# Attention and an MLP on one core: chunks of the MLP that follow the batches, and a first batch whose weights stay fp32

## The chip, the cores and the metric

The kernel runs on one core of a Trainium2 chip. TensorE (PE) multiplies, VectorE (DVE), ScalarE (ACT) and GpSimd (POOL) work elementwise, and SyncE (SP) issues all DMAs of this kernel. The metric is the device time of one launch in microseconds; the change is judged by the median of several runs before against several after.

## The reference

Attention over 8 batches with 8 heads, 576 tokens and 64 columns a head, in which all weights below the row's maximum less tau are set to zero; then an MLP over the 4608 rows of 512 columns:

```python
scores = scale * np.matmul(q, k.transpose(0, 1, 3, 2))
thresh = np.max(scores, axis=-1, keepdims=True) - tau
scores = np.where(scores >= thresh, scores, -1000000000.0)
scores = scores - np.max(scores, axis=-1, keepdims=True)
attn = np.exp(scores)
attn = attn / (np.sum(attn, axis=-1, keepdims=True) + 1e-09)
x = (attn @ v)              # to rows: (batch, token), columns: (head, 64)
h = x @ w_in                # 512 -> 2048
g = np.maximum(h, 0.0) + np.log1p(np.exp(-np.abs(h)))
out = g @ w_out             # 2048 -> 512
```

The two MLP weights arrive in 64-bit floats, q, k and v in 32-bit.

## The kernel before

**Units and tiles.** Two heads of one batch are a unit (32 units, four to a batch). A unit's scores are nine tiles of 128 query rows by 576 keys: four of the first 512 rows of each head, and one in the middle (tile 4) that holds the last 64 rows of both heads. The main loop (line 873) runs over the 288 tiles; within one it takes the steps of the string PAT in order, a letter each: high half, row maximum of the next tile, low half, transposes, exp, a part of the MLP, mask, another part, the extras, the scores of the tile after next, weight preparation, and the point at which deferred functions run. A function that is deferred by n runs at the n-th such point.

**One tile.** PE computes scores into one of two PSUM pairs (`scores`); DVE takes the row maximum (`row_max`), ACT the exp (`exps`), DVE applies the mask and sums the row (`mask`). POOL writes the weights' high half in fp16 (`weights_hi`, line 452), DVE the low half (`weights_lo`, line 457), and a DMA transposes both halves (`weights_T`); the halves lie in one of three buffers, `e16`. When a head is complete, PE multiplies the transposed halves by v, which is also split in two fp16 halves after a scaling (`top_v`, `split_v`, `values`); ACT and DVE add the two parts into `xp` (`values_out`). One unit's row sums become scales `R`, are written to DRAM and read back on 64 partitions each, POOL multiplies `xp` by them (`scale_x`, line 513), and three DMAs store it in DRAM (`store_x`). The q and k of the next unit are split in two parts, transposed on PE and copied by ACT on the way (`pre`).

**The MLP.** A chunk is 512 consecutive rows, nine in all, so a chunk straddles batches. `load_x` fetches it from DRAM, `split_x` scales it (ACT) and makes two fp16 halves (POOL). `hidden` (line 584) multiplies with w_in in three products (high by high, low by high, high by low), ACT computes softplus for two blocks at a time behind a table load, POOL splits the result into halves `g`, and `project` (line 646) multiplies with w_out; DVE adds the quarters of it up in `acc`. A generator, `stream`, yields after every matmul: one 512-column matmul is one unit of work, a chunk is 384 units. `target` says how many units are due at each tile: chunk 0 from tile 43, the next from 82, 118 and so on, one chunk for 36 tiles, 10.7 units a tile. Chunks 7 and 8 come after the last tile; they are called the tail and may use buffers that attention no longer needs.

**The weights.** Each of 32 pieces of 128 x 512 is read as words, one every second tile from tile 0. ACT, POOL and DVE turn them into fp32 (`to_f32`), DVE takes the maximum of each piece (`got`), four pieces make a block whose maximum gives its scale (`over_all`), then ACT scales and POOL splits it (`split`).

**Order.** DVE and ACT keep the program's order from tile 72 on (TQ); before that a scheduler orders the instructions of each engine. PE has four general PSUM banks (`ps_g`) for everything but the scores.

Of the kernel before, what the change touches and what calls it, by code (L numbers as in the profile page):

```python
# [24 lines left out]
P = 128  # L25
# [7 lines left out]
LAG0 = 7  # L33
PAT = "hRlTefmpfxSwp"
# [8 lines left out]
NW = 34  # L43
EB = 3
EXP = 0x7F800000
LAG = 10
NMM = 11.0
# [10 lines left out]
def tile_kernel(ctx: ExitStack, tc: tile.TileContext, q, k, v, tau, w_in, w_out, out):  # L58
# [53 lines left out]
    x_d = [dpool.tile([P, NPAIR, S], F32, name=f"x_d{b}") for b in range(B)]  # L112
# [60 lines left out]
    def over_all(name, cols, then):  # L173

        col = cpool.tile([P, 1], F32, tag="col", bufs=3, name=f"col_{name}")
        vec.reduce_max(col, cols, axis=AX.X)
# [18 lines left out]
    def to_f32(src, name, then):  # L195
# [21 lines left out]
        def second(m, n):  # L217
            mu = m.bitcast(U32)
            if n == 0:
                i = vec.tensor_scalar(out=mu, in0=mu, scalar1=3, scalar2=None, op0=ALU.logical_shift_left)  # L220
            elif n == 1:
# [27 lines left out]
    def prep_w(kind, g, n):  # L249

        ms, tops = blocks.setdefault((kind, g), ([], cpool.tile([P, 4], F32, tag="tops", bufs=3, name=f"tops_{kind}{g}")
                                                 if n == 0 else None))
# [27 lines left out]
        to_f32(src, f"{kind}{g}_{n}", got)  # L280
# [13 lines left out]
    for b in range(B):  # L294
        for hp in range(NPAIR):
            s = Unit()
            s.i, s.b, s.hp = len(units), b, hp
            s.r_d = dpool.tile([9, P], F32, name=f"r_d{s.i}")
            units.append(s)

    def load(s):
        h0 = 2 * s.hp
        s.kn = apool.tile([P, 10, D], F32, tag="nat", bufs=3, name=f"kn_{s.i}")
        s.qn = apool.tile([P, 10, D], F32, tag="nat", bufs=3, name=f"qn_{s.i}")
        for t, src in ((s.kn, k), (s.qn, q)):
            nc.sync.dma_start(
                t.rearrange("p (h s) d -> p h (s d)", h=2)[:, :, 0:NC * D],
                src[s.b, h0:h0 + 2, 0:SM, :].rearrange("h (p c) d -> p h (c d)", c=NC),
            )
# [15 lines left out]
    def top_v(s):  # L325
        tops = cpool.tile([P, 1], F32, tag="vtop", bufs=2, name=f"vtop_{s.i}")
        vec.tensor_reduce(tops, s.vn[0:P].rearrange("p h s d -> p (h s d)"), axis=AX.X, op=ALU.max,
                          apply_absolute_value=True)
# [12 lines left out]
        defer(1, spread)  # L341

    def split_v(s, j):
        if j == 0:
# [5 lines left out]
    def split_k(s):  # L350
# [3 lines left out]
        s.q2, s.kT, s.qT = [], [], []  # L354
# [87 lines left out]

    def mask(s, t):
# [3 lines left out]
            accum_out=s.sums[:, t:t + 1]))  # L447
# [12 lines left out]
    def weights_T(s, t):  # L460
# [4 lines left out]
        if t == M:  # L465
            nc.sync.dma_start_transpose(s.eT[0][:, :, SM:S], h[0:SR])
            nc.sync.dma_start_transpose(s.eT[1][:, :, 0:SR], h[SR:P])
            return
        j, c = divmod(t, NC + 1)
        c0 = j * SR + c * P  # L470
        nc.sync.dma_start_transpose(s.eT[j][:, :, c0:c0 + P], h)

    def values(s, g):
        if g == 0:
            s.xp = apool.tile([P, S], F32, tag="xp", name=f"xp_{s.i}")
# [15 lines left out]
    def row_scales(s):  # L491
        s.rs = apool.tile([P, 9], F32, tag="rs", name=f"rs_{s.i}")
        vec.tensor_scalar(out=s.rs, in0=s.sums, scalar1=1e-9, scalar2=v_scale[:, s.i:s.i + 1], op0=ALU.add, op1=ALU.mult)
# [7 lines left out]
    def row_scales_out(s, ps):  # L501
        rt = apool.tile([P, S], F32, tag="R", bufs=1, name=f"rt_{s.i}")[0:9, 0:P]
        act.activation(rt, ps[0:9, 0:P], AF.Copy, scale=2.0 ** -15)
        nc.sync.dma_start(s.r_d, rt)
        s.R = apool.tile([P, S], F32, tag="R", bufs=1, name=f"R_{s.i}")
        rows = s.r_d.rearrange("a p -> (a p)")
        for j in range(2):
            nc.sync.dma_start(s.R[j * D:(j + 1) * D, :], rows[j * S:(j + 1) * S].partition_broadcast(D))
        defer(XD, lambda: scale_x(s))
        defer(XD + 2, lambda: store_x(s))  # L510

    def scale_x(s):
        nc.gpsimd.tensor_tensor(out=s.xp, in0=s.xp, in1=s.R, op=ALU.mult)

    def store_x(s):
        for j, c0, n, t0 in ((0, 0, S, 0), (1, SR, SM, 0), (1, 0, SR, SM)):
            nc.sync.dma_start(x_d[s.b][j * D:(j + 1) * D, s.hp, t0:t0 + n], s.xp[j * D:(j + 1) * D, c0:c0 + n])
        ready.add(("x", s.b, s.hp))
# [5 lines left out]
    def load_x(u, cc):  # L524
        st = fpool.tile([P, TC], F32, tag="xst", name=f"xst_{u.n}_{cc}")
        u.st[cc] = st
        c = 0
        while c < u.T:
            b, o = divmod(u.t0 + c, S)
            m = min(S - o, u.T - c)  # L530
            need("x", b, cc)
            nc.sync.dma_start(st[:, c:c + m], x_d[b][:, cc, o:o + m])
            c += m

    def x_scale(u):
        n = NPAIR * ((u.t0 + u.T - 1) // S + 1)
        for i in range(n):
            need("v", i)
# [4 lines left out]
        vec.tensor_reduce(u.sx, v_scale[:, 0:n], axis=AX.X, op=ALU.min)  # L543
# [22 lines left out]
    def split_x(u, cc):  # L566
        if cc % 2 == 0:
            for l, tag in ((u.h, "xh"), (u.l, "xl")):
                t = fpool.tile([P, 2 * TC], F16, tag=tag, name=f"{tag}_{u.n}_{cc}")
                l += [t[:, i * TC:(i + 1) * TC] for i in range(2)]  # L570
        st = u.st.pop(cc)
# [3 lines left out]
    def hidden(u, fc):  # L575
# [4 lines left out]
        bank = ps_g.tile([P, TC], F32, tag="g", name=f"h_{u.n}_{fc}")  # L580
        e = slice(f * P, (f + 1) * P)
        for cc in range(NCC):
            for m, (i, x) in enumerate(((0, u.h), (0, u.l), (1, u.h))):
                nc.tensor.matmul(bank, wi[g, cc][:, i, e], x[cc], start=(cc == 0 and m == 0),  # L584
                                 stop=(cc == NCC - 1 and m == 2))
                if cc == NCC - 1 and m == 2:
                    u.full.append((fc, bank))
# [3 lines left out]
                yield 1.0  # L591
# [27 lines left out]
    def parts_of(u, fc, t):  # L619

        pool, tags, bufs = (fpool, ("gh", "gl"), NG)
        if u.tail:
            spare = [("kT", 2), ("qT0", 2), ("qT1", 2), ("nat", 3), ("e16", EB)]
# [7 lines left out]
        u.g[fc] = (gh, gl)  # L631
# [35 lines left out]
    def store_out(u, tb, a):  # L667
        t0 = u.t0 + tb * P
        c = 0
        while c < P:  # L670
            b, o = divmod(t0 + c, S)
            if o < SM:
                cg, p0 = divmod(o, P)
                m = min(P - p0, P - c)
                dst = out[b * S:b * S + SM, :].rearrange("(p c) e -> p c e", c=NC)[p0:p0 + m, cg, :]
            else:
                m = min(S - o, P - c)
                dst = out[b * S + o:b * S + o + m, :]
            nc.sync.dma_start(dst, a[c:c + m, :])
            c += m  # L680
# [29 lines left out]
    def stream():  # L710
# [4 lines left out]
        for it in order():  # L715
# [7 lines left out]
            if it[2:4] == (0 if u.tail else nq - 2, 0) and u.n + 1 < len(chunks):  # L723
                x_scale(chunks[u.n + 1])
            if it[4] >= 0:
# [7 lines left out]
                if it[4] == 0:  # L733
                    load_x(nx, 0)
# [32 lines left out]
    chunks, first = [], []  # L767
    while sum(u.T for u in chunks) < NT:
        u = Chunk()
        u.n, u.t0 = len(chunks), sum(c.T for c in chunks)  # L770
        u.T = TC
        u.h, u.l, u.acc, u.g, u.st, u.full = [], [], [], {}, {}, []
        u.scaled, u.unscaled = set(), set()
        b, o = divmod(u.t0 + u.T - 1, S)
        first.append((b + 1) * 9 * NPAIR + (LAG if chunks else LAG0))
        u.tail = first[-1] >= NS
# [3 lines left out]
    def target(g):  # L780

        done = 0
        for n, u in enumerate(chunks):
            work = 3 * NFC * (NCC * u.T / 512 + u.T / P)
            end = first[n + 1] if n + 1 < len(chunks) else 1 << 30
            if g < end:
                rate = work / (end - first[n])
                if n + 2 >= len(chunks) or end == first[n]:
                    rate = NMM
                return done + max(0, min(work, (g - first[n]) * rate))  # L790
            done += work
# [20 lines left out]
    def extras(i, t):  # L812
# [4 lines left out]
        for g, at_ in enumerate(VO):  # L817
            if at_ == t:
                values(cur, g)
            if at_ == 9 + t and prev:  # L820
                values(prev, g)
# [16 lines left out]
    for s in units:  # L838
        if s.i == 0:
            times = ((0, -1), (0, 0), (0, 3), (0, 4))  # L840
        elif s.i == 1:
            times = ((0, 4), (0, 6), (0, 8), (1, 0))
# [27 lines left out]
    scores(*tiles[1])  # L870

    done = 0.0
    for g, (cur, t) in enumerate(tiles):
# [6 lines left out]
        for step in PAT:  # L880
            if step == "T" and g:
                weights_T(*tiles[g - 1])
            elif step == "h":
                weights_hi(cur, t)
            elif step == "l" and g:
                weights_lo(*tiles[g - 1])
            elif step == "R" and nxt:
# [11 lines left out]
            elif step == "S" and g + 2 < NS:  # L899
                scores(*tiles[g + 2])  # L900
            elif step == "w":
# [46 lines left out]
```

## Time and profile before

| | |
|---|---|
| median of 3 runs | 1506.12 us (1504.12 to 1508.0) |
| the profiled execution | 1502.2 us |
| its span, first to last instruction | 1500.4 us |
| mean granted TensorE clock | 0.939 |
| DMA, share of 16 engines | 57.7% |

Durations and shares are of the profiled execution; its time is 1.8 us more than its span. A row of a view by windows gives, for a stretch of the span, its length, then for each engine the busy time and, in brackets, how many instructions ran, the granted clock, the share of time in which the DMA engines were busy, and the GB/s. A row of a group gives the line, the engine, the operation, what it writes and reads, the shape and the count; then the busy time and the mean of one in ns; then the idle time of the engine just before these instructions and who ended it. Line 147 is a helper through which all DVE and ACT operations pass, so those are told apart by names and shapes. A row of the waits gives who waited for whom, the time in all, how often and the longest.

### The profile page before, as it was taken

The numbers are of one execution on the slowest core, as the hardware profiler recorded it, in microseconds if no ns is written. First come the engines' busy times: TensorE is split into PE (matmuls) and PEld (weight loads), VectorE is DVE, ScalarE is ACT, GpSimd is POOL, SyncE is SP. The second block draws the span as 40 slices with busy tenths as digits, with TensorE's granted clock in tenths as the row PEclk, the third lists the DMA queues.
The fourth block names the chain that finished last, engine by engine and source line by source line (L and its number), as shares of the span: only waits on it lengthen the run. The fifth ranks groups of instructions, "written<-read, shape, count | busy, mean of one in ns | idle before, by whom it ended". The sixth has DMA issues, their size and how long they took to land.

```text
span 1500.4 us, 21721 instructions
## 1 busy us (share of the span) xinstructions
PE 1241.6 (83%) x6608; PEld 719.2 (48%) x6608; DVE 1062.1 (71%) x2113; ACT 819.9 (55%) x1305; POOL 987.9 (66%) x1097
## 2 busy tenths in 40 slices
PE   4554557877989988998898888998989889999998
PEld 3432334544555545554555545554555445444443
DVE  7897998998877887777777777787777767610101
ACT  4433446656566656665565656665766576442231
POOL 5477788887776667666766676667766775353531
PEclk9755659999999999999999999999999999999999
DMA  5877876755576656666765586666665756420101
GB/s 158 182 154 179 178 170 161 176 136 132 128 168 132 143 141 161 141 141 136 167 140 126 142 173 148 128 139 157 153 134 138 161 131 126 95 65 1 37 7 28
DMA packets 445317, 199.30 MB, mean 133 GB/s; under 512 B 376048, under 2 KB 419344, under 8 KB 445200
## 3 DMA queue, kind: packets, MB, share of 16 engines
q1 hardware_dynamic: 445200, 197.90, 57.7%
q8 instruction: 53, 0.87, 0.2%
q14 instruction: 64, 0.52, 0.1%
HBM read 73.40 MB, written 19.02 MB: 62 GB/s over the span
## 4 chain that ended last, share of the span: by engine, by line
DVE 24%; ACT 20%; PE 18%; issue 10%; POOL 10%; DMA 8%; SPq 3%; ACTq 0%; POOLq 0%; DVEq 0%
PE o L646 7%; PE h L584 7%; DVE negm L147 6%; DVE e_all L147 6%; ACT st L147 6%; ACT e_all L147 6%; ACT L147 5%; DMA eT<-e 3%; DVE e L147 3%; DVE acc L147 2%; DVE xp L147 2%; DMA vn<-in_v_dram 2%; PE s L429 2%; PE pv L480 1%; POOL g L171 1%
## 5 line engine op out<-in xcount | busy, mean ns | idle before, releaser
L646 PE MATMUL o<-w_o,g 128*128 128x512 f16 x1728 | 413.8, 384 | 21.6 <-POOL g L170 14.5
L452 POOL TENSOR_SCALAR e<-e_all 128x576 f16<-128x576 f32 x288 | 232.6, 808 | 279.0 <-DMA eT<-e 207.1
L147 ACT ACTIVATE e_all<-s,negm 128x576 f32<-128x576 f32 x288 | 213.0, 741 | 316.8 <-DVE negm L147 290.7
L584 PE MATMUL h<-xh,w_i 128*128 128x512 f16 x1152 | 374.2, 385 | 6.4 <-POOL xh L170 2.9
L429 PE MATMUL s<-kT,qT 128*128 128x288 f32 x1024 | 244.2, 354 | 119.4 <-DVE e_all L147 108.0
L147 DVE SCALAR_TENSOR_TENSOR e_all<-s,thr,e_all 128x576 f32<-128x576 f32 x288 | 233.7, 812 | 112.1 <-ACT e_all L147 111.6
L147 DVE SCALAR_TENSOR_TENSOR e<-e_all,e 128x576 f16<-128x576 f32 x288 | 276.9, 961 | 15.3 <-POOL e L452 14.2
L646 PEld LDWEIGHTS <-g 128*128 128x128 f16 x1728 | 158.7, 99 | 207.5 <-POOL g L170 20.1
L584 PEld LDWEIGHTS <-w_i 128*128 128x128 f16 x1728 | 161.0, 99 | 190.3 <-issue 17.8
L429 PEld LDWEIGHTS s<-kT,qT 128*128 128x128 f32 x1024 | 168.9, 208 | 172.4 <-DVE e_all L147 145.6
L147 DVE TENSOR_REDUCE negm<-s 128x1 f32<-128x576 f32 x288 | 215.5, 748 | 19.3 <-PE s L429 17.5
L584 PE MATMUL h<-xl,w_i 128*128 128x512 f16 x576 | 221.3, 384 | 4.8 <-POOL xl L171 4.8
L147 DVE SCALAR_TENSOR_TENSOR acc<-o,c,acc 128x512 f32<-128x512 f32 x108 | 79.6, 738 | 166.1 <-PE o L646 133.2
L480 PE MATMUL pv<-eT,vt 128*128 128x288 f16 x1152 | 179.6, 305 | 7.6 <-DMA eT<-e 6.8
L171 POOL TENSOR_TENSOR g<-st,g 128x512 f16<-128x512 f32 x144 | 169.9, 1181 | 8.3
L170 POOL TENSOR_SCALAR g<-st 128x512 f16<-128x512 f32 x144 | 99.9, 695 | 98.5 <-ACT st L147 96.2
L147 ACT ACT_TABLE_LOAD x109 | 139.8, 1283 | 27.6 <-DVE negm L147 26.0
L480 PEld LDWEIGHTS <-vt 128*128 128x128 f16 x1152 | 116.7, 104 | 64.4 <-issue 8.3
L147 ACT ACTIVATE st<-h,c 128x512 f32<-128x512 f32 x144 | 91.2, 684 | 87.6 <-PE h L584 87.0
L147 DVE TENSOR_TENSOR xp<-pv,xp 64x288 f32<-64x288 f32 x128 | 57.6, 450 | 94.9 <-ACT xp L147 93.2
L147 ACT ACTIVATE st<-st,c 128x512 f32<-128x512 f32 x144 | 96.1, 715 | 2.1
L171 POOL TENSOR_TENSOR vt<-vn,vt 128x576 f16<-128x576 f32 x64 | 84.6, 1321 | 1.8
(90 smaller groups left out, 1356.4 us busy)
## 6 DMA issues: line engine op xcount, KB each, us to landing
vn<-in_v_dram SPq DMA_DIRECT2D x128, 128.0 KB
qT<-qT SPq DMA_DIRECT2D x124, 128.0 KB
R<-r_d SPq DMA_DIRECT2D x64, 144.0 KB
kn<-in_k_dram SPq DMA_DIRECT2D x32, 256.0 KB
qn<-in_q_dram SPq DMA_DIRECT2D x32, 256.0 KB
wc_i<-in_moe_w_in_dram SPq DMA_DIRECT2D x16, 512.0 KB
wc_o<-in_moe_w_out_dram SPq DMA_DIRECT2D x16, 512.0 KB
eT<-e SPq DMA_TRANSPOSE x320
```

What stands on the lines that cost most here:

```text
L147: i = getattr(self.eng, name)(*args, **kwargs)
L170: nc.gpsimd.tensor_scalar(out=hi, in0=x, scalar1=1.0, scalar2=1.0, op0=ALU.mult, op1=ALU.mult)
L171: nc.gpsimd.tensor_tensor(out=lo, in0=x, in1=hi, op=ALU.subtract)
L429: nc.tensor.matmul(sp[:, hf, 0:HS], lhs, s.kT[j][:, hf * HS:(hf + 1) * HS], start=(m == 0), stop=(m == len(parts) - 1))
L452: nc.gpsimd.tensor_scalar(out=h[:, :, 0, :], in0=s.e[t].rearrange("p (c n) -> p c n", n=SR), scalar1=2.0 ** 15, scalar2=1.0, op0=ALU.mult, ...
L480: nc.tensor.matmul(o[:, 0:HS], s.vt[:, j, slot, :], s.eT[j][:, c, x0:x0 + HS], start=(c == 0), stop=(c == 8))
L584: nc.tensor.matmul(bank, wi[g, cc][:, i, e], x[cc], start=(cc == 0 and m == 0), stop=(cc == NCC - 1 and m == 2))
L646: nc.tensor.matmul(o, u.g[fc][m // 2][:, sl], wo[fc][:, m % 2, :], start=(n == 0), stop=(n == 3 * QF - 1))
```

## The change

- **Chunks.** A main chunk is the first 512 tokens of one batch. `xp` stays in SBUF (five buffers in place of two) and `split_x` reads it there. The last 64 tokens of four batches make a rest chunk of 256 rows, the only part that still goes through DRAM. There are eight main chunks and two rest chunks, each with its due tile written out: main chunks at 42, 80, 116, 152, 188 and 224, the first rest chunk at 252, the seventh batch's chunk at 265, the eighth's at 293 and the last rest chunk at 330. Those with 288 or more are the tail.
- **Batch 0 whole.** For its four units the weights stay in fp32: PE transposes them in five blocks (`whole_T`), ACT copies them to SBUF in place (`whole_copy`), and PE multiplies them in fp32 with v as it is loaded (`whole_values`, whose products run three at a time in a new step `v` of PAT). High and low halves, DMA transposes, the split of v and the addition of two parts go for these units.
- **Weight pieces.** For the 64-bit weights POOL adds up the four pieces of a block elementwise (`add`), and DVE takes one maximum of the sum, in place of a maximum of each piece. The scale comes from this larger bound.
- **Buffers.** From tile 84 on every second tile's fp16 halves go into the three buffers that the weight words no longer need, so there are six for three. q and k have two buffers for three, the pieces 33 for 34.
- **Order.** R is read one point later than it is written, and in four DMAs for two; the middle tile's row sums come last.

The core of it:

```diff
-LAG0 = 7
-PAT = "hRlTefmpfxSwp"
+LAG0 = 6
+PAT = "hRlTefmpfxSvwp"
-NW = 34
+NW = 33
+NF = 4
+NX = 5
+TE = 84
+VW = (2, 5, 7, 9)
+QB = 4
-LAG = 10
-NMM = 11.0
+LAG = 8
...
         def got(m):
-            vec.reduce_max(tops[:, n:n + 1], m, axis=AX.X, apply_absolute_value=True)
             ms.append(m)
-            if len(ms) == 4:
-                over_all(f"{kind}{g}", tops, scaled)
+            if src.dtype == F32:
+                vec.tensor_tensor(out=tops[0], in0=tops[0] if n else m, in1=m, op=ALU.abs_max)
+            if n == 3:
+                over_all(f"{kind}{g}", tops[0], scaled)
+        def add(m):
+            if n:
+                nc.gpsimd.tensor_tensor(out=tops[0], in0=tops[0], in1=m, op=ALU.add)
+            else:
+                nc.gpsimd.tensor_scalar(out=tops[0], in0=m, scalar1=1.0, scalar2=1.0, op0=ALU.mult, op1=ALU.mult)
...
-        s.kn = apool.tile([P, 10, D], F32, tag="nat", bufs=3, name=f"kn_{s.i}")
+        s.kn = apool.tile([P, 10, D], F32, tag="nat", bufs=2, name=f"kn_{s.i}")
...
+    def whole_T(s, t):
+        e = s.e.pop(t)
+        main = ps_g.tile([P, NC, P], F32, tag="g", name=f"tm_{s.i}_{t}")
+        rest = ps_g.tile([P, NC, P], F32, tag="g", name=f"tr_{s.i}_{t}")[0:SR, 0, :]
+        for c in range(NC):
+            nc.tensor.transpose(main[:, c, :], e[:, SR + c * P:SR + (c + 1) * P], ident)
+        nc.tensor.transpose(rest, e[:, 0:SR], ident)
+    def whole_copy(s, t):
+        main, rest = s.e16.pop(t)
+        for g, c, c0, n in place[t]:
...
+            act.copy(h[:, 0:NC, c:c + n], main[:, :, c0:c0 + n])
+            act.copy(h[0:SR, NC, c:c + n], rest[:, c0:c0 + n])
+    def whole_values(s, g):
...
+        n = 320 if g in (1, 2) else 256
...
+        def product(c):
+            k_ = slice(0, P if c < NC else SR)
+            nc.tensor.matmul(o[0:D, 0:n], s.vn[k_, 5 * j + c, :], h[k_, c, 0:n], start=(c == 0), stop=(c == NC))
...
+        slow.extend([lambda c=c: product(c) for c in range(NC + 1)])
...
     def weights_hi(s, t):
-        s.e16[t] = h = apool.tile([P, 9, 2, SR], F16, tag="e16", bufs=EB, name=f"e16_{s.i}_{t}")
+        pool, tag, bufs = (apool, "e16", EB) if now["tile"] < TE or t % 2 else (wpool, "wi", WB)
+        s.e16[t] = h = pool.tile([P, 9, 2, SR], F16, tag=tag, bufs=bufs, name=f"e16_{s.i}_{t}")
...
     def store_x(s):
-        for j, c0, n, t0 in ((0, 0, S, 0), (1, SR, SM, 0), (1, 0, SR, SM)):
-            nc.sync.dma_start(x_d[s.b][j * D:(j + 1) * D, s.hp, t0:t0 + n], s.xp[j * D:(j + 1) * D, c0:c0 + n])
+        n = s.b % QB
+        nc.sync.dma_start(x_d[s.b // QB][:, s.hp, n * SR:(n + 1) * SR], s.xp[:, SM:S])
...
+        if u.main:
+            need("x", NPAIR * u.b + cc)
+            st = units[NPAIR * u.b + cc].xp[:, 0:SM]
+        else:
+            st = u.st.pop(cc)
...
+    spans = ((1, 0, 36 + LAG0), (1, 1, 72 + LAG), (1, 2, 108 + LAG), (1, 3, 144 + LAG), (1, 4, 180 + LAG), (1, 5, 216 + LAG),
+             (0, 0, 252), (1, 6, 265), (1, 7, 293), (0, 1, 330))
...
+        u.T = SM if main else QB * SR
...
+        for u, nx in zip(chunks, chunks[1:]):
             work = 3 * NFC * (NCC * u.T / 512 + u.T / P)
...
+            done += work * min(1, max(0, (g - u.from_) / (nx.from_ - u.from_)))
```

In `spans` each entry says whether the chunk is a main one, which batch (or which four batches) it covers, and the tile from which it is due.

More of the change, by code (lines that the diff above doesn't have):

```diff
@@ L111, in tile_kernel @@
     p_w = {kind: cpool.tile([P, NFC // 4], F32, name=f"p_{kind}") for kind in "io"}
-    x_d = [dpool.tile([P, NPAIR, S], F32, name=f"x_d{b}") for b in range(B)]
+    x_d = [dpool.tile([P, NPAIR, QB * SR], F32, name=f"x_d{n}") for n in range(B // QB)]
     qm = cpool.tile([P, 2, 2, P], F32R, name="qm")
@@ L193, in piece, with to_f32 @@
         return cpool.tile(shape, dt, tag="w", bufs=NW, name=name)
-    def to_f32(src, name, then):
+    def to_f32(src, name, size, then):
         while reading[0] >= WB or live[0] + 2 > NW:
@@ L492, in row_scales @@
         s.rs = apool.tile([P, 9], F32, tag="rs", name=f"rs_{s.i}")
-        vec.tensor_scalar(out=s.rs, in0=s.sums, scalar1=1e-9, scalar2=v_scale[:, s.i:s.i + 1], op0=ALU.add, op1=ALU.mult)
+        if s.whole:
+            vec.tensor_scalar(out=s.rs, in0=s.sums, scalar1=1e-9, scalar2=None, op0=ALU.add)
+        else:
+            vec.tensor_scalar(out=s.rs, in0=s.sums, scalar1=1e-9, scalar2=v_scale[:, s.i:s.i + 1],
+                              op0=ALU.add, op1=ALU.mult)
         vec.reciprocal(s.rs, s.rs)
@@ L630, in parts_of @@
         halves(gh, gl, t)
-        u.g[fc] = (gh, gl)
+        for i in range(TC // u.T):
+            c = slice(i * u.T, (i + 1) * u.T)
+            u.g[fc + i] = (gh[:, c], gl[:, c])
     def project(u, qt, tb):
@@ L667, in store_out @@
     def store_out(u, tb, a):
[L668 to L680, printed above, removed]
+        if u.main:
+            dst = out[u.b * S:u.b * S + SM, :].rearrange("(p c) e -> p c e", c=NC)[:, tb, :]
+            nc.sync.dma_start(dst, a)
+            return
+        for i in range(2):
+            r = (QB * u.b + 2 * tb + i) * S + SM
+            nc.sync.dma_start(out[r:r + SR, :], a[i * SR:(i + 1) * SR, :])
     nq = NFC // QF
@@ L816, in extras @@
         prev = units[i - 1] if i else None
[L817 to L821, printed above, removed]
+        for s, t_ in ((prev, t + 9), (cur, t)):
+            if s and t_ in (VW if s.whole else VO):
+                (whole_values if s.whole else values)(s, (VW if s.whole else VO).index(t_))
         if t == RT and prev:
@@ L870, in tile_kernel @@
     scores(*tiles[1])
+    load_v(units[1])
     done = 0.0
@@ L880, in tile_kernel @@
         for step in PAT:
-            if step == "T" and g:
-                weights_T(*tiles[g - 1])
-            elif step == "h":
+            if step == "T":
+                if cur.whole:
+                    whole_T(cur, t)
+                if g and not tiles[g - 1][0].whole:
+                    weights_T(*tiles[g - 1])
+            elif step == "h" and not cur.whole:
                 weights_hi(cur, t)
-            elif step == "l" and g:
+            elif step == "l" and g and not tiles[g - 1][0].whole:
                 weights_lo(*tiles[g - 1])
+            elif step == "m" and cur.whole:
+                whole_copy(cur, t)
+                mask(*nxt)
             elif step == "R" and nxt:
```

170 lines of the change are left out of this document (107 added, 63 removed).

## The prediction

> **What bounds the kernel now.** I read the page's totals first, then the busy time by stage, then the groups and waits of single stages.
>
> ```profile
> span 1500.4 us, 21721 instructions
> core 0: us, PE busy (x) PEld busy (x) DVE busy (x) ACT busy (x) POOL busy (x), PEclk, DMA share, GB/s
> 14.00:185.00 171.00, 88.40 (x388) 66.58 (x387) 150.84 (x298) 69.83 (x126) 120.12 (x129) 0.68 0.75 174
> 185.00:424.00 239.00, 181.58 (x936) 108.92 (x937) 210.72 (x423) 136.11 (x220) 192.29 (x206) 0.87 0.65 152
> 424.00:1027.00 603.00, 533.17 (x3005) 311.11 (x3002) 460.00 (x921) 381.94 (x596) 413.23 (x463) 0.99 0.65 145
> 1027.00:1297.00 270.00, 240.47 (x1357) 141.02 (x1358) 203.98 (x414) 167.62 (x259) 181.23 (x205) 0.99 0.62 140
> 1297.00:1500.40 203.40, 193.96 (x904) 87.97 (x903) 31.24 (x51) 59.40 (x94) 79.49 (x90) 1.00 0.12 31
> ```
>
> I cut the span where batches end. The same windows for the row maxima and the exp that reads them count the attention tiles (ACT's count: one exp per tile):
>
> ```profile
> 14.00:185.00 171.00, 34.28 (x73) 26.35 (x36) 0.68 0.75 174
> 185.00:424.00 239.00, 45.99 (x98) 36.21 (x49) 0.87 0.65 152
> 424.00:1027.00 603.00, 134.81 (x280) 103.77 (x140) 0.99 0.65 145
> 1027.00:1297.00 270.00, 60.69 (x126) 46.69 (x63) 0.99 0.62 140
> ```
>
> So there are five stages. Batch 0 (36 tiles) takes 4.75 us a tile with DVE 88% busy: attention and weight preparation share DVE, and PE has no MLP work yet. The next 49 tiles take 4.9 us each, DVE 88%, POOL 80%. The 140 tiles after them take 4.31 us with PE 88%; the last 63 take 4.29 us with PE 89%. The end, 203 us, is MLP alone with PE at 95%. What is moved out of the end into the attention costs nothing only as far as PE has gaps there.
>
> **The tail and the last attention tiles.** A unit of MLP work is one 512-column matmul; 48 of them take 10.36 us in the chain of waits, so 0.216 us each. The windows for line 584 (hidden) and line 646 (output), in that order, count them:
>
> ```profile
> 1464.64 10.36 PE h L584 x48
> 1027.00:1297.00 270.00, 86.39 (x360) 32.84 (x360) 0.99 0.62 140
> 1297.00:1500.40 203.40, 90.16 (x408) 39.89 (x408) 1.00 0.12 31
> 1027.00:1297.00 270.00, 78.02 (x324) 28.81 (x325) 0.99 0.62 140
> 1297.00:1500.40 203.40, 103.15 (x468) 45.51 (x467) 1.00 0.12 31
> ```
>
> A full chunk is 384 units, nine are 3456; 408 + 468 = 876 are left when attention ends. By the new due times six main chunks (2304) are done by tile 252, the 192 units of the first rest chunk by 265, and the seventh batch's chunk, due from 265 to 293, has 23/28 of 384 = 315 done at tile 288: 2811 done, 645 left. So 231 units leave the end: 231 x 0.216 = 50 us. I take 7 us off for new seams: the rest chunk splits all four pieces of the next chunk in its last 12 units, and the last chunk has two short quarters behind its softplus. **End: -43 us** (-50 to -36).
>
> Of the 231, about 22 go to tiles 36 to 84 (first chunk due at 42 and second at 80, in place of 43 and 82). The other 207 land in the last 63 tiles: 684 + 207 = 891 units, about 14 per tile in place of 10.7. That is 207 x 0.216 = 44.7 us of PE in a stage whose PE is idle 270 - 240 = 30 us. All gaps used: +15. PE kept at 89%: 44.7 / 0.89 = +50. I take half of the gaps, +30, and 4 us for the seam: **last tiles +34 us** (+15 to +50).
>
> **Batch 0 kept whole.** The groups of that stage:
>
> ```profile
> L147 DVE SCALAR_TENSOR_TENSOR e<-e_all,e 128x576 f16<-128x576 f32 x34 | 33.3, 979 | 0.2
> L452 POOL TENSOR_SCALAR e<-e_all 128x576 f16<-128x576 f32 x36 | 35.1, 977 | 24.9 <-DVE e_all L147 10.2 <-DMA eT<-e 9.0 <-DVE col_o L147 3.1
> L171 POOL TENSOR_TENSOR vt<-vn,vt 128x576 f16<-128x576 f32 x10 | 13.9, 1389 | 0.8
> L170 POOL TENSOR_SCALAR vt<-vn 128x576 f16<-128x576 f32 x10 | 8.3, 828 | 2.5 <-ACT vn L147 2.4
> L147 ACT ACTIVATE vn<-vn,v_scale 128x576 f32<-128x576 f32 x10 | 7.5, 768 | 2.4 <-issue 1.8 <-DVE v_scale L147 0.6
> L147 DVE TENSOR_REDUCE tops_i<-wa_i 128x1 f32<-128x512 f32 x11 | 7.4, 672 | 0.0
> L147 DVE TENSOR_TENSOR xp<-pv,xp 64x288 f32<-64x288 f32 x13 | 5.8, 444 | 0.2
> ```
>
> DVE loses the low half (33.3 us) and the value adds (5.8). Weight pieces start every second tile, so some 15 reductions of 672 ns fall here (10 us), and 4 of about that size, one per block, stay: -7.4. DVE: 150.8 - 46.5 = 104 us. POOL loses 35.1 and eight tenths of 22.2, and gains the sums of the weight pieces. Those, and the copies ACT gains, have these neighbours over the whole run:
>
> ```profile
> L513 POOL TENSOR_TENSOR xp<-xp,R 128x576 f32<-128x576 f32 x32 | 47.1, 1473 | 40.6 <-DMA R<-r_d 32.2 <-DVE topv L147 5.3 <-DVE negm L147 1.6
> L214 POOL TENSOR_SCALAR wa_o<-wa_o 128x512 f32<-128x512 f32 x16 | 11.5, 717 | 5.7 <-ACT wa_o L147 4.6
> L147 ACT CAST kT<-tr 128x512 fp32r<-128x512 f32 x64 | 37.3, 583 | 12.2 <-PE s L429 10.6 <-PE tr L376 0.9
> L147 ACT CAST kT<-tr 128x64 fp32r<-128x64 f32 x64 | 13.5, 210 | 20.2 <-PE tr L371 17.7 <-PE tr L369 1.8
> L147 ACT COPY xp<-pv 64x288 f32<-64x288 f32 x128 | 50.3, 394 | 57.1 <-PE pv L480 54.7
> ```
>
> A two-input sum over 512 columns is 1473 x 512/576 = 1.31 us, so a block of four costs POOL 0.72 + 3 x 1.31 = 4.65 us; here +17, POOL 85 us. ACT per tile: 0.583 + 0.210 (the middle tile in two parts, 2 x (0.39 + 0.21)): 7.5 us per unit, 30 for four. Output copies are five in place of four (+1.6); the scaling of v goes (-6). ACT: 95 us.
>
> PE's new form is whole fp32. Two places in the timeline of PE price it by the start of what follows (a bare start, a duration, the group):
>
> ```profile
> 1245.89 0.39 PE L332 MATMUL topv<-identr,vtop 128*128 128x128 f32 x2
> 1246.11 0.38 PE L584 MATMUL h<-xh,w_i 128*128 128x512 f16 x1
> 1303.23 0.28 PE L498 MATMUL rT<-identr,rs 128*9 128x128 f32 x1
> 1303.35 1.46 PE L646 MATMUL o<-w_o,g 128*128 128x512 f16 x6
> 1298.80 1.12 PE pv L480 x9
> ```
>
> One fp32 product of 128 columns runs as two instructions, 0.22 us together, 1.72 ns a column; an fp32 transpose is one, 0.12 us. A unit has 45 transposes (5.4 us) and 5 x (256 + 320 + 320 + 256) = 5760 columns of products (9.9 us); it sheds 36 products of 1.12/9 = 0.124 us (4.5 us). Four units: +43 us at full clock. The stage's present PE time is 88.4 at clock 0.68, some 60 us at full clock; after: 103. Whether that fits depends on the clock, which follows the load:
>
> ```profile
> 120.00:160.00 40.00, 19.44 (x88) 14.17 (x88) 32.89 (x67) 15.29 (x28) 26.10 (x29) 0.59 0.70 166
> 240.00:280.00 40.00, 32.79 (x173) 19.55 (x172) 36.01 (x73) 29.69 (x48) 35.34 (x38) 0.91 0.60 144
> ```
>
> PE 49% busy had 0.59, 82% had 0.91. 103 us in about 125 is 82%, so I take 0.91: 113 us.
>
> So DVE has 104 us, PE 113, ACT 95, POOL 85. DVE at today's 88% gives 118. With three engines that near each other, handing every tile round, I take 128: 3.55 us a tile. **Batch 0: -43 us** (-53 to -21). Queued behind the new waits: the tile's transposes stand in PE's order ahead of later scores and wait for the mask and for two of the four general PSUM banks, which ACT frees by its copies. A third and fourth bank are left for q and k transposes and for one value product, so I put no extra wait there. The first loads of unit 1 now wait for unit 0's q and k to be split (two buffers for three); they are due a tile or more later.
>
> **Tiles 36 to 84.** Two things add: POOL's sums of the other four blocks (4 x 4.65 = 18.6 us; POOL was 80% busy) and 22 units x 0.216 = 5 us of PE; one thing goes: 17 reductions less 4 (-9 us) on DVE, which was 88% busy. The sums wait one block for the next too, since one buffer is left for them. Between -9 and +24 I take **+8**.
>
> **Tiles 84 to 224.** Here the extra buffers count:
>
> ```profile
> POOL e L452 <- DMA eT<-e: 134.5, 58, 5.6
> PEld L646 <- POOL g L170: 14.6, 8, 3.0
> ACT e_all L147 <- POOL e L452: 13.8, 6, 3.6
> ACT xst L147 <- DMA xst<-x_d: 11.7, 6, 3.7
> ```
>
> POOL stood 134.5 us of 603 before a high half, waiting for a transpose to free one of three buffers; three more, used by every second tile, end most of it. POOL is 69% busy, so only what others waited for in turn counts: PE for POOL's halves 14.6, ACT's exp 13.8, and the chunk's way through DRAM 11.7, which main chunks no longer take. Together 40 us, on three engines whose waits overlap; nothing of it at the least. I take **-18** (0 to -42). SP's queue gets shorter: per unit one x store for three, four loads of R for two; per run 8 chunk loads for 64 and 40 fewer transposes. The five xp buffers bind only if a chunk's split came more than a tile late.
>
> **Sum.** -43 + 8 - 18 + 34 - 43 = -62 us. The profiled execution took 1502.2 us (1.8 around the span), so 1440; the median of the runs shown is 1506.1, 3.9 above it, so **1444 us**.
>
> **Rivals.** 1. *The last stage is full.* PE stays at 89% (+50 in place of +34) and the e buffers were no bound (0 in place of -18): 1478. For it: PE is the busiest engine there, and what is named above is small waits. Against: in the end PE reaches 95%.
> 2. *The buffers were the bound.* The 140 tiles go to 533 / 0.95 = 561 us (-42) and the last stage takes the work into its gaps (+15): 1401. For it: 134.5 us of waiting; against: few waited for POOL in turn.
> 3. *Batch 0 becomes bound by PE* (slower). If the clock stays at about 0.62, 103 us become 166, and if the waits below stay beside them, the stage takes 213, +42 in place of -43: 1529. It decides when the stage's clock stays under about 0.7. For it: that is where the clock stands today; against: the two rows of the clock above, by which 103 us of work in 125 lift it.
>
> ```profile
> PE s L429 <- DVE e_all L147: 46.6, 23, 3.3
> ```
>
> The Trainium skill speaks for this rival ("TensorE: Matmul & The Clock Gate", Part 4: PE-mode transpose): a transpose does not count as PE activity for the clock in the same way as a matmul. Of the 103 us, 22 are transposes of the new kind; by that page only 81 would lift the clock, and the stage would lie between the forecast and this rival, some 20 us above the forecast. The trace of before has too few such transposes to show it.
>
> 4. *It doesn't do what it says*: splits forced early or sums on POOL hold up SP and POOL, so that two of the gains fail at once: about 1505.
>
> **How the numbers follow.** Forecast 0.52 (its own range 1425 to 1465), first rival 0.20, second 0.13, third 0.10, fourth 0.05. The range takes in the first two and leaves the others out: 1398 to 1492. Faster by over 0.3% (what a measurement can tell from no change): 0.84, within 0.3%: 0.05, slower: 0.11.
>
> **What would show it.** Right: 36 tiles in about 128 us with the clock near 0.9; the wait of POOL for the transposes nearly gone after tile 84; 4.7 to 4.9 us a tile with PE over 92% at the last 63; some 645 units and 160 us in the end. Wrong: batch 0 at its old time with ACT or PE full; an end that begins 50 us later than it would by this sum; POOL over 90% in tiles 36 to 84 with PE waiting for it.

## The result and the profile after

The change takes the kernel from 1505.1 to 1439.2 us (medians of four runs each), a ratio of 0.956, with a 95% interval from 0.954 to 0.958. The 1506.1 us ahead of the prediction is the median of three of these four runs of before. The forecast was 1444. The profiled execution took 1442.1 us, so the profiles differ by 60 us where the medians differ by 66. Its first line, and then its busy time by stage (the stages end where the same tiles end as before: 36, 49, 140 and 63, then the end):

```profile
span 1440.3 us, 22136 instructions
core 0: us, PE busy (x) PEld busy (x) DVE busy (x) ACT busy (x) POOL busy (x), PEclk, DMA share, GB/s
14.00:152.00 138.00, 111.54 (x569) 76.19 (x570) 104.40 (x242) 88.03 (x200) 85.10 (x94) 0.90 0.42 120
152.00:402.00 250.00, 191.52 (x973) 113.35 (x972) 205.97 (x395) 139.86 (x229) 213.75 (x224) 0.88 0.62 137
402.00:994.00 592.00, 529.97 (x3015) 310.67 (x3014) 454.30 (x922) 378.85 (x593) 406.91 (x465) 1.00 0.64 133
994.00:1291.00 297.00, 278.18 (x1644) 168.86 (x1643) 207.42 (x423) 193.85 (x292) 190.52 (x226) 1.00 0.55 117
1291.00:1440.30 149.30, 144.21 (x775) 75.51 (x772) 24.25 (x46) 44.89 (x71) 58.89 (x70) 1.00 0.10 28
```

The second column of each row is the length of the stage. Beside the lengths before (171, 239, 603, 270, 203) and beside the steps of the prediction:

| stage | predicted | measured |
|---|---|---|
| batch 0, 36 tiles | -43 | -33 |
| next 49 tiles | +8 | +11 |
| next 140 tiles | -18 | -11 |
| last 63 tiles | +34 | +27 |
| the end | -43 | -54 |
| sum | -62 | -60 |

Every sign is right and the sum is off by 2 us, but single terms are off by up to 11: that they cancel is luck. The experiments show that one term, the 140 tiles, came near for a wrong reason, and that another, batch 0, left out a cost. In the 140 tiles, POOL waits in the changed kernel as the first two rows say; the last two are waits of others for POOL:

```profile
POOL e L541 <- DVE e_all L151: 77.2, 49, 2.4
POOL q L124 <- DMA qn<-in_q_dram: 29.5, 14, 3.7
ACT e_all L151 <- POOL e L541: 19.8, 13, 2.5
PEld L754 <- POOL g L174: 4.3, 4, 1.1
```

The 134.5 us of waiting for a transpose are gone. In their place POOL waits for the mask, the next thing that comes last, and there is a wait that the kernel before did not have: for the loads of q. Of the three small waits that the prediction added up, the one for the chunk's way through DRAM is gone and PE's for POOL's halves fell from 14.6 to 4.3 us, but ACT's for POOL rose from 13.8 to 19.8. On the chain of work that ended last, by engine and by line on the page, POOL now has the largest share, 24% where it had 10%, and these loads 2% of the span, some 29 us:

```profile
POOL 24%; PE 22%; DVE 15%; ACT 15%; issue 13%; DMA 7%; SPq 4%; POOLq 0%; ACTq 0%; DVEq 0%
PE o L754 8%; PE h L690 7%; ACT L151 5%; POOL e L541 4%; ACT st L151 4%; DVE e_all L151 4%; ACT e_all L151 4%; DVE negm L151 3%; PE s L458 3%; POOL vt L175 2%; DMA qn<-in_q_dram 2%; POOL xl L175 2%; POOL vt L174 2%; DMA R<-r_d 2%; PE pv L568 1%
```

### The profile page after: what moved, and what is told of

The parts are those of the page before. It is cut to its first block, busy times and chain, and to the rows that moved or that the text cites. A ratio compares the mean times of both kernels' runs of the same rounds, so it can differ in the third digit from the quotient of the medians.

```text
span 1440.3 us, 22136 instructions
## 1 busy us (share of the span) xinstructions
PE 1261.3 (88%) x6996; PEld 749.1 (52%) x6996; DVE 1003.5 (70%) x2035; ACT 851.0 (59%) x1395; POOL 958.2 (67%) x1085
## 4 chain that ended last, share of the span: by engine, by line
POOL 24%; PE 22%; DVE 15%; ACT 15%; issue 13%; DMA 7%; SPq 4%; POOLq 0%; ACTq 0%; DVEq 0%
PE o L754 8%; PE h L690 7%; ACT L151 5%; POOL e L541 4%; ACT st L151 4%; DVE e_all L151 4%; ACT e_all L151 4%; DVE negm L151 3%; PE s L458 3%; POOL vt L175 2%; DMA qn<-in_q_dram 2%; POOL xl L175 2%; POOL vt L174 2%; DMA R<-r_d 2%; PE pv L568 1%
## 5 line engine op out<-in xcount | busy, mean ns | idle before, releaser
L690 PE MATMUL h<-xh,w_i 128*128 128x512 f16 (+1 forms) x1280 | 366.8, 362 | 3.7 <-ACT st L151 2.6
L458 PE MATMUL s<-kT,qT 128*128 128x288 f32 x1024 | 227.3, 336 | 65.5 <-DVE e_all L151 63.0
L541 POOL TENSOR_SCALAR e<-e_all 128x576 f16<-128x576 f32 x252 | 183.4, 728 | 146.4 <-DVE e_all L151 136.0
L690 PEld LDWEIGHTS <-w_i 128*128 128x128 f16 x1920 | 179.7, 99 | 175.6 <-issue 18.0
L151 DVE SCALAR_TENSOR_TENSOR e<-e_all,e 128x576 f16<-128x576 f32 x252 | 239.4, 950 | 21.9 <-POOL e L541 19.6
L690 PE MATMUL h<-xl,w_i 128*128 128x512 f16 (+1 forms) x640 | 232.3, 363 | 4.0 <-POOL xl L175 4.0
L458 PEld LDWEIGHTS s<-kT,qT 128*128 128x128 f32 x1024 | 158.4, 197 | 102.1 <-DVE e_all L151 89.1
L568 PE MATMUL pv<-eT,vt 128*128 128x288 f16 x1008 | 145.7, 291 | 8.6 <-DVE acc L151 4.5
L568 PEld LDWEIGHTS <-vt 128*128 128x128 f16 x1008 | 98.9, 99 | 54.6 <-issue 12.7
L175 POOL TENSOR_TENSOR vt<-vn,vt 128x576 f16<-128x576 f32 x56 | 73.2, 1308 | 1.3
```

The costliest lines, as they stand in the source:

```text
L151: i = getattr(self.eng, name)(*args, **kwargs)
L175: nc.gpsimd.tensor_tensor(out=lo, in0=x, in1=hi, op=ALU.subtract)
L458: nc.tensor.matmul(sp[:, hf, 0:HS], lhs, s.kT[j][:, hf * HS:(hf + 1) * HS], start=(m == 0), stop=(m == len(parts) - 1))
L541: nc.gpsimd.tensor_scalar(out=h[:, :, 0, :], in0=s.e[t].rearrange("p (c n) -> p c n", n=SR), scalar1=2.0 ** 15, scalar2=1.0, op0=ALU.mult, ...
L568: nc.tensor.matmul(o[:, 0:HS], s.vt[:, j, slot, :], s.eT[j][:, c, x0:x0 + HS], start=(c == 0), stop=(c == 8))
L690: nc.tensor.matmul(bank[:, i * u.T:(i + 1) * u.T], wi[g, cc][:, a, e], x[cc], start=(cc == 0 and m == 0), stop=(cc == NCC - 1 and m == 2))
```

## The experiments

Each was timed beside the kernel before. e1 to e5 and e8 differ from the changed kernel in one point each; e7 and e6 build on e4; e9 to e11 build on e6; e12 is the kernel before with one part of the change. Stage lengths below come from each kernel's own profile with the same tile counts.

**e1, batch 0 split again.**

```diff
-NF = 4
+NF = 0
```

The v loads of units 0 and 1 go back to their old places with it.

> Batch 0 is split in fp16 halves again, all else of the change stays. If the 32 us that batch 0's 36 tiles gained come from the whole weights (DVE without the low half, 104 us of work in place of 151), those tiles go back to about 170 us and the time to about 1470. Rival: the gain comes from the weight sums that left DVE and from fewer DMAs; then the 36 tiles stay under 150 us and the time under 1450.

1498.4 us, ratio to the kernel before 0.995 (0.993 to 0.997): 59 us lost, nearly the whole change. The stage is longer than it was before the change:

```profile
14.00:198.00 184.00, 86.76 (x389) 66.36 (x387) 154.38 (x283) 69.41 (x126) 138.55 (x142) 0.67 0.69 152
```

Both expectations missed: the whole weights are worth 46 us here, but 13 of them only make up for something else in the change that costs time when batch 0 is split. POOL has 138.6 us where it had 120.1. That pointed at the sums.

**e2, three buffers for the fp16 halves.**

```diff
-TE = 84
+TE = 999
```

> The fp16 halves have three buffers all along, all else of the change stays. If POOL's wait for the transposes was what the 140 middle tiles lost, it comes back (over 100 us of POOL's idle time), those tiles go from 593 to about 607 us, the last 63 get some us longer too, and the time goes to about 1455. Rival: POOL's wait held nobody else up and the 14 us come from the x that stays in SBUF; then the time stays within 5 us of 1439.

1446.1 us (0.960, 0.956 to 0.964), 7 us more than with six, though the two intervals overlap a little. POOL's wait is back for a good part:

```profile
POOL e L541 <- DMA eT<-e: 69.2, 33, 4.2
399.00:997.00 598.00, 532.44 (x3019) 311.56 (x3018) 461.03 (x926) 378.82 (x593) 412.94 (x465) 1.00 0.64 132
```

69 us of POOL's idle time stand beside 6 us more in the 140 tiles. Neither the 14 us of the expectation came nor the rival's nothing. Six us are near the limit of what one profile can tell: in the change, e1, e3, e4, e5, e7 and e8, whose work in these tiles is the same, the stage takes 592 to 597 us.

**e3, the rest chunks after attention.** Some 200 units go back to the end.

```diff
-             (0, 0, 252), (1, 6, 265), (1, 7, 293), (0, 1, 330))
+             (1, 6, 260), (1, 7, 296), (0, 0, 315), (0, 1, 330))
```

> Both rest chunks come after attention, the seventh batch's chunk is due at 260 and the eighth's at 296, so that some 850 units are left at the end as before the change. If PE's gaps in the last 63 tiles took part of the moved work, the end grows by about 45 us, the last tiles shrink by about 30, and the time goes to about 1455. Rival: that stage was full, work costs the same at both places, and the time stays at 1439 (within 4 us).

1461.2 us (0.969, 0.966 to 0.972). The last tiles and the end:

```profile
994.00:1259.00 265.00, 238.38 (x1350) 139.32 (x1349) 199.82 (x407) 170.22 (x262) 175.71 (x201) 1.00 0.60 126
1259.00:1459.00 200.00, 188.75 (x1063) 103.66 (x1062) 31.29 (x59) 58.67 (x94) 77.69 (x94) 1.00 0.10 27
```

The moved work costs 297 - 265 = 32 us in the last tiles and 200 - 149 = 51 us at the end. PE's busy time in the last tiles rises by 40 us in 32 us more, so 8 us of gaps were filled. The expectation had 30, 45 and a time of 1455 us: the mechanism came as expected, with a somewhat larger gain.

**e4, the maxima on DVE again.** DVE takes the maximum of each piece, POOL adds nothing up, and the sum's buffer of 512 columns becomes one of four.

```diff
-            tops.append(cpool.tile([P, DM], F32, tag="tops", bufs=1, name=f"tops_{kind}{g}"))
+            tops.append(cpool.tile([P, 4], F32, tag="tops", bufs=3, name=f"tops_{kind}{g}"))
...
+            vec.reduce_max(tops[0][:, n:n + 1], m, axis=AX.X, apply_absolute_value=True)
...
         def add(m):
-
-            if n:
-                nc.gpsimd.tensor_tensor(out=tops[0], in0=tops[0], in1=m, op=ALU.add)
-            else:
-                nc.gpsimd.tensor_scalar(out=tops[0], in0=m, scalar1=1.0, scalar2=1.0, op0=ALU.mult, op1=ALU.mult)
+            return
```

> The maxima of the weight pieces are taken on DVE again, POOL adds nothing up. If POOL's sums are what made tiles 36 to 84 10 us longer, these go from 250 to about 240 us, batch 0 stays, and the time is about 1430. Rival: DVE is the tighter engine; its 17 us of reductions come back in batch 0 and in tiles 36 to 84, and the time is about 1450.

1422.3 us (0.944, 0.942 to 0.946), 17 us faster than the change (23 us between the profiled executions):

```profile
14.00:142.00 128.00, 107.80 (x573) 73.51 (x573) 110.60 (x254) 85.94 (x198) 66.11 (x74) 0.93 0.46 129
142.00:378.00 236.00, 188.37 (x963) 110.55 (x963) 207.36 (x415) 141.34 (x231) 202.94 (x212) 0.88 0.66 145
```

Batch 0, which the expectation left as it was, takes 128 us in place of 138, the next tiles 236 in place of 250. DVE has 6 us more to do in batch 0 and the stage is 10 us shorter: an engine's busy time doesn't say what its work costs. The mean of a sum on POOL was near what the prediction had taken, 1.27 us for 1.31. The first row is from batch 0 of the changed kernel, the second, DVE's addition of two operands of the same size, from its page:

```profile
L270 POOL TENSOR_TENSOR tops_i<-tops_i,wa_i 128x512 f32<-128x512 f32 x9 | 11.5, 1273 | 12.0 <-DVE wa_i L151 6.2 <-DVE p_i L151 5.8
L151 DVE SCALAR_TENSOR_TENSOR acc<-o,c,acc 128x512 f32<-128x512 f32 x108 | 80.0, 743 | 119.7 <-ACT st L151 60.7
```

The last columns of the first row point at the rest of the price. Each sum stands between two steps of DVE on the same piece, and POOL stood idle 12 us in front of these nine for DVE's steps. The Trainium skill ("GPSIMD Engine Reference", 4.1 Engine selection) sends elementwise sums and maxima to VectorE, since two-input operations on GpSimd are about half as fast. This case agrees in the main: 1273 ns a sum on POOL against 743 ns on DVE, 1.7 times as long. (The maximum that the sum replaced reads one input and took 672 ns.)

**e5, a second place for the sums.** The change has one buffer for them, so neighbouring blocks wait for each other. Three of the eight blocks get a free piece buffer.

```diff
-            tops.append(cpool.tile([P, DM], F32, tag="tops", bufs=1, name=f"tops_{kind}{g}"))
+            own = (kind, g) in (("i", 1), ("i", 2), ("i", 3))
+            tops.append(piece([P, DM], F32, f"tops_{kind}{g}") if own else
+                        cpool.tile([P, DM], F32, tag="tops", bufs=1, name=f"tops_{kind}{g}"))
```

> POOL still adds the weight pieces up, but three of the eight blocks keep their sum in a free piece buffer, so that neighbouring blocks no longer wait for the one sum buffer. If that wait is what cost the 23 us that the maxima on DVE regained, batch 0 goes from 137 to about 127 us, the 49 tiles after it from 250 to about 238, the time to about 1418. Rival: it is POOL's own work, 1.27 us a sum in line with everything else that POOL does; then the stages stay and the time is 1439 within 4 us.

1440.9 us (0.956, 0.955 to 0.958): no difference from the change, as the rival had it. The single buffer is not the cause; the sums on POOL themselves are what is left.

**e6, a third buffer for q and k.** The room of e4's sum buffer lets q and k have their three buffers back.

```diff
-        s.kn = apool.tile([P, 10, D], F32, tag="nat", bufs=2, name=f"kn_{s.i}")
+        s.kn = apool.tile([P, 10, D], F32, tag="nat", bufs=3, name=f"kn_{s.i}")
```

The same for qn; at the end the tail may use all three.

> Maxima on DVE, and in the room of the sum buffer the third buffer for q and k. If POOL's new wait for the q loads (29.5 us in the 140 middle tiles) comes from the second buffer alone and holds others up, the middle tiles go from 594 to about 580 us and the time from 1422 to about 1408. Rival: POOL takes the split of q earlier than anyone needs it, and the time stays at 1422 within 4 us.

1398.2 us (0.928, 0.926 to 0.929): 24 us under e4 and 41 under the change, the fastest kernel here, and 10 us more gained than expected. In the 140 tiles POOL's split of q no longer waits for the loads, but for PE, a shorter time; the second row is that stage, the third the chain by engine:

```profile
POOL q L124 <- PE tr L400: 21.4, 12, 2.0
377.00:952.00 575.00, 527.65 (x3016) 312.25 (x3015) 447.27 (x924) 378.84 (x593) 409.43 (x465) 1.00 0.66 137
PE 29%; DVE 22%; ACT 16%; issue 12%; POOL 11%; DMA 6%; SPq 3%; ACTq 0%; POOLq 0%; DVEq 0%
```

575 us in place of 592 in the change and 594 in e4, and POOL is no longer the largest part of the chain. The whole difference between the profiled executions of e4 and e6, 19 us, lies in this stage. PE is busy 2 us less than in the change and DVE 7 us less, so nearly all of the gain is waiting. One more buffer, which took 29.5 us of POOL's waiting away and left 21.4 of another, gained 17 to 19 us, although POOL was only 69% busy. In POOL's order the MLP's halves and the weights' high halves stand behind the split of q; that this is the way the wait reached PE was read from the order, not tried by itself. Nor was the buffer of k tried apart from that of q.

**e7, batch 1 whole as well** (on e4).

```diff
-NF = 4
+NF = 8
```

> Maxima on DVE, and batch 1 whole as well. It adds about 43 us of PE work to tiles 36 to 72, where PE already has the first chunk of the MLP, and takes some 40 us from DVE. If DVE is still what binds there, the 49 tiles go from 236 to about 225 us and the time to about 1411. Rival: PE and its four general banks, two of which a whole tile holds, bind as soon as the MLP runs beside; then these tiles take 250 us or more and the time is 1437 or more.

1420.9 us (0.943, 0.942 to 0.945), no difference from e4 that the runs show; neither of the two expectations came.

```profile
141.00:380.00 239.00, 222.63 (x1171) 130.43 (x1170) 162.24 (x364) 159.88 (x307) 138.78 (x160) 0.97 0.37 94
```

DVE loses 45 us of 207, and the stage stays at 239: PE goes from 80 to 93% busy. So in this batch, where PE has the MLP beside them, whole weights gained nothing.

**e8, each transpose of batch 0 made twice.**

```diff
+        for _ in range(2):
             for c in range(NC):
                 nc.tensor.transpose(main[:, c, :], e[:, SR + c * P:SR + (c + 1) * P], ident)
             nc.tensor.transpose(rest, e[:, 0:SR], ident)
```

> Each transpose of batch 0 on PE is made twice, 22 us more of PE work in these 36 tiles. If PE binds batch 0, they go from 137 to 155 us or more and the time to about 1458. Rival, that DVE, PE and ACT hand the tile round and none is full: a third to a half of it, 1446 to 1450. If transposes count for the clock, its mean in this stage rises from 0.90 to 0.95 or more; if they don't, it stays or falls, since the counted work is spread over a longer time.

1450.2 us (0.962, 0.961 to 0.964).

```profile
14.00:160.00 146.00, 125.15 (x745) 90.53 (x746) 107.40 (x244) 88.03 (x200) 87.40 (x95) 0.94 0.40 114
```

22 us of PE work, by the prediction's price of a transpose, cost 8 us in the stage and 11 in the time, about as the rival had it; PE's busy time rose by 13.6 us. PE is close to the bound in batch 0, but not the bound. The clock rose from 0.90 to 0.94 although the work that is no transpose was spread over a longer time. In the change, e2, e3 and e5, whose batch 0 is the same but for e5's buffers, it is 0.89 to 0.91.

**e9, three buffers for the fp16 halves** (on e6).

```diff
-TE = 84
+TE = 999
```

> Like e6 (maxima on DVE, three buffers for q and k, 1398 us), but the fp16 halves have three buffers all along. If the late q loads had hidden the worth of the six buffers, the middle tiles go from 575 to about 590 us and the time to about 1415. Rival: they are worth the 5 to 7 us that e2 showed, wherever they are taken away; then about 1405.

1402.2 us (0.931, 0.929 to 0.933), 4 us more than e6.

```profile
POOL e L536 <- DMA eT<-e: 83.6, 38, 4.8
372.00:950.00 578.00, 529.42 (x3017) 313.51 (x3015) 452.85 (x924) 378.49 (x593) 411.32 (x465) 0.99 0.66 137
```

83.6 us of POOL's waiting stand beside 3 us more in the stage, as little as two profiles of the same work differ by (e2). So the late q loads had hidden little or nothing, and the rival's 1405 us came nearest. The two intervals all but touch, and the profiled execution here is the shorter one (a span of 1396.4 us against 1398.5), so these 4 us are near the limit of what the runs can tell.

**e10, batch 0 split** (on e6), with the old places of the first v loads.

```diff
-NF = 4
+NF = 0
```

> Like e6, but batch 0 is split in fp16 halves again, now with the maxima on DVE as before the change. If the whole weights are worth 43 us by themselves, the 36 tiles go from 128 to about 170 us and the time to about 1441. Rival: in e1 it was the sums on POOL that made the split batch so slow, and in the change they were hidden by the whole weights; then the 36 tiles take 160 us or less.

1452.4 us (0.966, 0.965 to 0.967), 54 us more than e6.

```profile
14.00:189.00 175.00, 89.27 (x389) 66.97 (x387) 150.38 (x299) 69.83 (x126) 121.50 (x129) 0.68 0.72 162
```

Without the sums the split stage takes 175 us, near the 171 of before, and 128 whole: 47 us, where 43 were expected. Some 8 more are lost in the stage behind it (243 us for 235).

**e11, due times spread over 100 tiles** (on e6).

```diff
-             (0, 0, 252), (1, 6, 265), (1, 7, 293), (0, 1, 330))
+             (0, 0, 217), (1, 5, 230), (1, 6, 260), (1, 7, 293), (0, 1, 330))
```

> Like e6, but the first rest chunk comes between the fifth and the sixth batch's, so that the extra work begins at tile 188 and lies more evenly: 12 to 15 units a tile over 100 tiles in place of 14 over 63. If PE's gaps in the middle tiles take work more cheaply than the full last tiles, the last 63 tiles lose 10 us or more, the middle ones gain 5 or less, and the time is about 1392. Rival: a unit costs the same 0.15 us in both stages; then the time stays at 1398 within 4 us.

1406.1 us (0.934, 0.933 to 0.936), 8 us slower than e6, which neither expectation had.

```profile
372.00:974.00 602.00, 555.58 (x3221) 333.29 (x3220) 453.89 (x932) 394.23 (x613) 417.21 (x481) 0.99 0.64 134
974.00:1255.00 281.00, 259.35 (x1458) 151.84 (x1457) 207.82 (x413) 177.53 (x273) 178.43 (x210) 0.99 0.56 117
```

The last tiles lose 16 us as hoped, but the 140 tiles gain 27, with 28 us more of PE time: there PE's gaps take nothing at all. A likely reason is that e6 had left little to fill: by these rows PE's idle time is 0.34 us a tile in the 140 tiles of e6 and 0.33 here, 0.42 in the last tiles of e3, which lack the moved work, and 0.30 in those of the change, which have it. No run tried this by itself.

**e12, the kernel before with six buffers.**

```diff
-        s.e16[t] = h = apool.tile([P, 9, 2, SR], F16, tag="e16", bufs=EB, name=f"e16_{s.i}_{t}")
+        pool, tag, bufs = (apool, "e16", EB) if now["tile"] < 84 or t % 2 else (wpool, "wi", WB)
+        s.e16[t] = h = pool.tile([P, 9, 2, SR], F16, tag=tag, bufs=bufs, name=f"e16_{s.i}_{t}")
```

> The kernel before with one part of the change: six buffers for the fp16 halves from tile 84 on. If POOL's wait for the transposes (134.5 us in the middle tiles) held up others there, the 607 us of the middle tiles become about 590 and the time 1485. Rival, after e2: it is worth 5 to 9 us, and the time is about 1498.

1498.2 us (0.995, 0.993 to 0.997): 8 us.

```profile
POOL e L453 <- DVE e_all L147: 119.2, 66, 2.4
ACT e_all L147 <- POOL e L453: 28.3, 15, 3.6
424.00:1024.00 600.00, 532.32 (x3022) 312.06 (x3020) 461.38 (x924) 382.93 (x598) 401.36 (x467) 1.00 0.69 146
1024.00:1289.00 265.00, 236.82 (x1337) 138.37 (x1335) 204.92 (x407) 165.68 (x257) 173.29 (x200) 0.99 0.65 140
```

The rival came. POOL's wait for the transposes turned into one for the mask, of nearly the same size, and the stage takes 600 us for 603 (the 607 of the expectation is not what the windows show). ACT's wait for POOL, of which the prediction counted 13.8 us as a gain to come, doubled. The last 63 tiles take 265 us for 270.

## Why the prediction was right, and where its steps were not

**The end and the last tiles: right, seams mis-sized.** The price of a unit held: in the end PE takes 10.36 us for 48 units, or 5.24 for 48 of half width, in the chain of waits:

```profile
1331.15 10.36 PE o L754 x48
1399.26 5.24 PE h L690 x48
1404.50 5.18 PE o L754 x24
```

The units came as counted: 651 instead of 645 are left for the end, a half-width matmul counted as half. I took 7 us off the end for new seams; PE waited 0.5 us in all for others there, and some 4 us of the old end's gaps went too (-54 for -43). In the last tiles I charged +34; by the windows it is +27, by e3, with the rest of the change in place, +32; the 5 us between them are as many as the six buffers take off these tiles in e12. The two steps together gave -9 and were -27.

**Batch 0: the mechanism right, a cost beside it put at nothing.** DVE was to have 104 us and has 104.4, PE 113 and has 111.5 at clock 0.90, POOL 85 and has 85.1; ACT has 88 for 95. The stage was to take 128 us, and in e4, without POOL's sums, it does. With them it takes 138. The step that failed is that the sums were priced by POOL's busy time alone, 17 us of the 85, and beyond that at nothing; they cost 10 us of the stage (e4). By the rows of e4, every sum lengthens a chain of steps on one weight piece that alternates between POOL and DVE. How the 10 us divide between POOL's delay and DVE's wait for the piece was not separated; e5 only rules the buffer out.

**Tiles 36 to 84: right.** +8 forecast, +11 measured, and e4 shows the cause: without the sums these tiles take 236 us, 3 less than before the change. POOL is 86% busy there, under the 90% that the prediction named as a sign of being wrong.

**Tiles 84 to 224: right by accident.** The step was -18 for the extra buffers, from the waits behind POOL, and for x that stays in SBUF. The buffers are worth 3 us of it in the kernel before (e12), 6 in the change (e2), 3 on e6 (e9), each near the limit of one profile. What the step left out cost 17 us (592 to 575 in e6): q and k with two buffers, which the prediction passed over with the remark that unit 1's first loads come a tile late. And something it took as a small part must have gained more: with three q and k buffers the stage falls from 603 to 575 us, and the buffers explain 3 to 6 of these 28. The rest lies in what no run took apart: x that stays in SBUF, the shorter queue of SP, chunks that end with batches, and the later reading of R, for which POOL waited 14.8 us in these tiles before, 25.3 in e12 and 1.8 in the change. No run put x back through DRAM or R back in its place, so this stays open. It also means that the forecast of 1444 was met with two costs that its sum did not hold, or not in full, the sums on POOL and the missing buffer: without them the kernel takes 1398 us (e6), below the prediction's own range.

**The rivals.** The last stage was not full (e3), the buffers were no bound (e2, e12), and the clock did not stay low: 0.90 in batch 0 where 0.68 was. The fourth was right that sums on POOL hold up others, but no two gains failed. On the clock the page of the Trainium skill named in the prediction ("TensorE: Matmul & The Clock Gate", Part 4: PE-mode transpose) and the trace differ: adding transposes alone lifted the granted clock from 0.90 to 0.94 (e8). The measurement decides: here transposes count enough, and the 20 us that the rule would have cost did not come; without the sums the stage took its 128 us at a clock of 0.93 (e4).

## What to carry to other kernels

The length of a wait does not tell what it costs; ask what stands behind it in its engine's order and what the engine will wait for next. Here 69 to 134 us of POOL waiting for transposes cost 8 us or less, while the missing buffer behind 29.5 us of waiting for q cost 17 or more. When an edit takes a buffer away to make room, price the loads that used it, and when it moves work to an engine with room, count the hand-overs that it adds to a chain, not the engine's busy time. Moving independent matmuls from a bare end into a stage with gaps on PE pays, here 32 us spent for 51 saved, but try the stage first: when the first rest chunk came 35 tiles earlier, its work filled no gap.

## What the runs showed of the hardware that was not expected

In these runs the granted clock of batch 0 rose with the whole of PE's busy time, fp32 transposes included: it was 0.68 with 88 us of PE busy in 171 (before), 0.90 with 112 in 138 (the change), and 0.94 with 125 in 146 when only transposes were added (e8), while the same 36 tiles split again were back at 0.68 (e10).
